# Feed-forward blocks 3 to 8 taken in pairs of 1024 tokens: Strassen products 512 columns wide

## The chip, the cores and the metric

The kernel runs on one NeuronCore of a Trainium2 chip. The metric is the device time of one execution in microseconds. Five engines work on it: TensorE (PE in the profile, its weight loads apart as PEld), VectorE (DVE), ScalarE (ACT), GpSimd (POOL) and SyncE (SP), which here only issues DMAs. POOL issues the DMAs that add into their target.

## The reference, cut to what matters

```python
# q, k, v: 8 batches x 8 heads x 576 x 64, float32
out_d = softmax(mean of 4 rows of q, k) @ mean of 4 rows of v, each row repeated 4 times
out_local = softmax of the scores with |i - j| < 4, else masked, @ v
x = out_d + out_local, as 8 x 576 x 512
mixed = real(fft(fft(x, axis=1), axis=2))
u = x + mixed
un = (u - mean(u)) / sqrt(var(u) + 1e-06)
ch = np.maximum(un @ w_ch1, 0.0) @ w_ch2      # 512 -> 2048 -> 512
return u + ch
```

The 8 x 576 = 4608 tokens are 9 blocks of 512. The last two lines, the feed-forward part, are where the change is.

## The kernel before, in words

**Order of the work.** Every step (a load, a reduction, a group of matmuls) is a small method that is registered by `at` and then run in the order of its place. A place comes from the table `TURNS`, one number for each call of a method, or, where the table has no more for it, from the time that the method `plan` gives. All the registered steps are emitted in one list, and each engine works its own part of this list in order. So the table and `plan` set each engine's queue; nothing is reordered later.

**Stages.** First comes attention and Fourier mixing of the 8 batches. It leaves three pieces of u in DRAM: `um` (mixed), `ux` (local attention) and `ud` (pooled attention). Feed-forward blocks 0 and 1 begin between its last steps. `Block.load` brings a tile of 128 tokens back: SP loads `um`, then POOL issues two adding DMAs, for `ux` (L1093) and `ud` (L1097). `stats` and `norm` make un on VectorE, with a power on POOL (L1108). `turn` transposes a tile on TensorE (four matmuls, L1123). `turn_high` copies it to fp32r on ScalarE (L1129), and `turn_low` leaves the rest on VectorE (L1132).

**Arithmetic.** Each float32 operand is a high fp32r part and a low rest, and a product is three matmuls: high by high, low by high, high by low. For a chunk f of 128 hidden units `first` needs 12 matmuls of 512 columns (L1256; 3 parts x 4 chunks of 128 channels). Then `high` makes hh = max(x, 0) in fp32r on ScalarE (L1260), `low` the rest hl on VectorE (L1264), and `second` adds 12 matmuls of 512 columns into four PSUM accumulators (L1276 to L1278). `hh` and `hl` have two buffers each. There are 16 chunks f, so 8 pairs of chunks, numbered j.

**Blocks 0 to 2** work like that. **Blocks 3 to 8** make the first layer of a pair j by Strassen's scheme in Winograd's form. The 512 tokens are two halves of 256 rows (a11, a12 the first half's two halves of channels, a21, a22 the second's). The weights' blocks b11, b21, b22 and the differences t1 to t4 lie in DRAM (`uw`, made once by `Differences`, L1036 to L1059), and `stream` loads the seven of a pair, 256 KB each, by SP (L1183). Of the tokens, `turn_copy` saves the transposed tile (L1144), `add_up` makes the four sums s1 to s4 on POOL (L1163), and `sum_high` and `sum_low` split them on ScalarE (L1174) and POOL (L1178). A `product` is 6 matmuls of 256 columns (L1194). `open` makes p1, p2 and p5, `more` adds to p1 and makes p7, `close` adds to p7 and makes p3: 42 matmuls for a pair. `save` copies p1 from PSUM twice (L1214), and `combine` makes five sums on VectorE (L1219), four of which are the hidden rows, in `rows`. A pair's `second` steps come one pair later. Between them stand the transposes of the next block. `finish` adds the accumulators to u (L1282).

## Time and profile before

| what | value |
|---|---|
| median of 3 runs | 1096.12 us (1089.71, 1096.12, 1096.14) |
| the profiled execution | 1093.14 us, its span 1091.2 us |
| TensorE | 1052.7 us busy, 9304 matmuls |
| VectorE, ScalarE, GpSimd | 620.4, 398.2, 333.2 us busy |
| granted TensorE clock, mean | 0.998 |
| DMA | 214.34 MB |

The span is from the first to the last instruction in the trace. The profiled execution's own time is 1.9 us longer, and 3.0 us under the median. A matmul's duration in the trace has its modelled end in it, and overlaps the next one's start, so the distance between starts tells what one costs.

### The profile page before, as it was taken

The page shows a single profiled execution, that of the slowest core. Times are in us where ns is not written, and L with a number is a line of the kernel's source. Part 1 is how long each engine was busy: PE and PEld are TensorE (multiplying, and loading weights), DVE is VectorE, ACT ScalarE, POOL GpSimd, SP SyncE. Part 2 cuts the span into 40 slices and gives each one's busy share as a digit, 9 for nine tenths or more (in the row PEclk, how much of TensorE's full clock was granted, in tenths as well). Part 3 has the DMA queues.
Part 4 walks back from the last instruction along what each step waited for, and adds up shares of the span by engine and source line. Part 5 has one row for each costly group of instructions (what it writes and reads, how often), then busy time and mean ns, then how long its engine had stood idle before and what let it go on. Part 6 is the DMA issues. An engine that isn't in the chain of part 4 may idle for free.

```text
span 1091.2 us, 24252 instructions
## 1 busy us (share of the span) xinstructions
PE 1052.7 (96%) x9304; PEld 887.5 (81%) x9304; DVE 620.4 (57%) x1298; ACT 398.2 (36%) x1113; POOL 333.2 (31%) x506
## 2 busy tenths in 40 slices
PE   8899989899989999999999999999999999999998
PEld 6667767677768888888888889898899889889997
DVE  6999888799886873432333534534534443353333
ACT  6775757765343441121231321231231232132121
POOL 1222232224644555644442222231140331231000
PEclk9999999999999999999999999999999999999999
DMA  8757688754835474756459457847945955975641
GB/s 325 245 176 235 222 224 260 231 159 159 201 107 164 137 222 144 175 149 146 144 190 308 153 187 197 277 153 220 300 156 170 307 171 164 256 245 165 222 155 38
DMA packets 121194, 214.34 MB, mean 196 GB/s; under 512 B 14432, under 2 KB 30720, under 8 KB 120952
## 3 DMA queue, kind: packets, MB, share of 16 engines
q1 hardware_dynamic: 110056, 191.96, 52.8%
q0 software_dynamic: 11024, 20.86, 10.6%
q8 instruction: 73, 1.20, 0.4%
q14 instruction: 41, 0.34, 0.1%
HBM read 166.81 MB, written 45.42 MB: 194 GB/s over the span
## 4 chain that ended last, share of the span: by engine, by line
PE 72%; DMA 12%; DVE 10%; issue 3%; ACT 2%; SPq 1%; POOL 1%; DVEq 0%; ACTq 0%; POOLq 0%
PE banks L1194 18%; PE banks L1276 11%; PE banks L1277 11%; PE banks L1278 11%; PE banks L1256 10%; PE banks L876 3%; DMA w1l<-ut 2%; DMA xa<-rest 1%; PE banks L916 1%; PE banks L1123 1%; DMA w1l<-ub 1%; DMA raw<-in_wq_dram 1%; DMA w1h<-ut 1%; DMA qkT<-in_qk_dram 1%; PE banks L767 1%
## 5 line engine op out<-in xcount | busy, mean ns | idle before, releaser
L1276 PE MATMUL banks<-w2h,hh 128*128 128x512 f32 x576 | 228.2, 396 | 0.0
L1277 PE MATMUL banks<-w2l,hh 128*128 128x512 f32 x576 | 225.5, 391 | 0.0
L1278 PE MATMUL banks<-w2h,hl 128*128 128x512 f32 x576 | 224.9, 390 | 0.2 <-DVE hl L1264 0.2
L1260 ACT ACTIVATE hh<-row 128x512 fp32r<-128x512 f32 x96 | 60.6, 632 | 282.5 <-DVE row L1219 190.9
L1219 DVE TENSOR_TENSOR row<-wt,banks 128x256 f32<-128x256 f32 x192 | 80.2, 418 | 140.1 <-PE banks L1194 135.5
L1264 DVE SCALAR_TENSOR_TENSOR hl<-row,hh 128x512 fp32r<-128x512 f32 x96 | 68.8, 717 | 118.7 <-ACT hh L1260 118.7
L1278 PEld LDWEIGHTS banks<-w2h,hl 128*128 128x128 f32 x576 | 108.2, 188 | 24.5 <-DVE hl L1264 0.7
L1276 PEld LDWEIGHTS banks<-w2h,hh 128*128 128x128 f32 x576 | 108.5, 188 | 19.7
L1277 PEld LDWEIGHTS banks<-w2l,hh 128*128 128x128 f32 x576 | 108.6, 188 | 19.1
L1256 PE MATMUL banks<-unT,w1h 128*128 128x512 f32 x384 | 102.2, 392 | 4.1 <-DVE unT L1132 2.6
L1256 PEld LDWEIGHTS banks<-unT,w1h 128*128 128x128 f32 x384 | 71.9, 188 | 20.7 <-DVE unT L1132 3.5
L1264 DVE SCALAR_TENSOR_TENSOR hl<-banks,hh 128x512 fp32r<-128x512 f32 x48 | 33.0, 687 | 85.6 <-ACT hh L1260 83.0
L1093 POOL DMA_DIRECT2D ut<-ux x40 | 36.6, 975 | 140.1 <-DMA ut<-um 129.8
L1260 ACT ACTIVATE hh<-banks 128x512 fp32r<-128x512 f32 x48 | 28.6, 595 | 115.3 <-PE banks L1277 96.0
L726 ACT ACTIVATE sb<-banks,mx 128x64 f32<-128x64 f32 x320 | 69.8, 329 | 2.1 <-PE banks L739 0.7
L1214 ACT COPY wt<-banks 128x256 f32<-128x256 f32 x96 | 35.7, 372 | 94.6 <-PE banks L1194 94.6
L876 PE MATMUL banks<-seq,f 128*128 128x290 f32 x256 | 67.4, 413 | 1.0 <-DVE odt L627 1.0
L1194 PE MATMUL banks<-w1h,w1l 128*128 128x256 f32 x384 | 62.6, 285 | 1.7 <-DMA w1l<-ut 0.9
L1194 PE MATMUL banks<-unT,w1h 128*128 128x256 f32 x432 | 63.4, 283 | 0.8 <-DVE row L1219 0.8
L1194 PEld LDWEIGHTS banks<-unT,w1h 128*128 128x128 f32 x432 | 59.8, 191 | 4.7 <-DVE row L1219 1.0
L1194 PE MATMUL banks<-w1h,w1h 128*128 128x256 f32 x384 | 61.8, 283 | 1.8 <-DMA w1h<-ut 1.7
L1194 PE MATMUL banks<-unT,w1l 128*128 128x256 f32 x432 | 63.2, 282 | 0.0
(117 smaller groups left out, 1891.8 us busy)
## 6 DMA issues: line engine op xcount, KB each, us to landing
w1h<-ut SPq DMA_DIRECT2D x96, 256.0 KB
w1l<-ut SPq DMA_DIRECT2D x96, 256.0 KB
qkT<-in_qk_dram SPq DMA_DIRECT2D x40, 512.0 KB
w1h<-ub SPq DMA_DIRECT2D x72, 256.0 KB
w1l<-ub SPq DMA_DIRECT2D x72, 256.0 KB
raw<-in_wq_dram SPq DMA_DIRECT2D x64, 256.0 KB
vaug<-in_vw_dram SPq DMA_DIRECT2D x40, 260.0 KB
out_dram<-ut SPq DMA_DIRECT2D x36, 256.0 KB
```

The costliest lines, as they stand in the source:

```text
L726: nc.scalar.activation(out=self.sb[:, hp, z], in_=self.sc[:, z, hp], func=AF.Exp, scale=0.125, bias=self.mx[:, z, hp : hp + 1],)
L876: nc.tensor.matmul(y, l, r, start=(i == 0), stop=(i == len(mms) - 1))
L1093: nc.gpsimd.dma_start(out=to, in_=ux[b][k0 : k0 + m, :], accum_op=ALU.add)
L1194: nc.tensor.matmul(into, w[:, y, c, :], both[z][:, c, :], start=(start and i == 0), stop=(i == len(mms) - 1), skip_group_check=True)
L1214: nc.scalar.copy(out=joins[k].bitcast(F32), in_=self.ps[x])
L1219: nc.vector.tensor_add(out=place(to), in0=place(a), in1=self.ps[x])
L1256: nc.tensor.matmul(hps, a[:, c, :], unT[:, x, c, :], start=(i == 0), stop=(i == len(mms) - 1))
L1260: nc.scalar.activation(out=hh, in_=self.hps[f], func=AF.Relu)
L1264: nc.vector.scalar_tensor_tensor(out=hl, in0=self.hps[f], scalar=0.0, in1=self.hh[f].bitcast(F32), op0=ALU.max, op1=ALU.subtract)
L1276: nc.tensor.matmul(acc, hh, w2h, start=start, stop=False)
L1277: nc.tensor.matmul(acc, hh, w2l, start=False, stop=False)
L1278: nc.tensor.matmul(acc, hl, w2h, start=False, stop=stop)
```

## The change

- Blocks 3 to 8 become three pairs (`Super`), each of two `Half` blocks: a, the first 512 tokens, is the upper row of the Strassen scheme, and b, the next 512, the lower. A product is again 6 matmuls, now of 512 columns, into a whole PSUM bank. `open` is split in two (`open` and `middle`).
- `combine` and `save` work on 512 columns. The hidden rows of a go on to `second` at once. Those of b are kept in DRAM (`uh`; `keep`, 256 KB each, for 14 of 16 chunks) and are fetched again (`fetch`) when a is finished; then the second layer of b runs as one stretch of 16 x 12 matmuls. For them there is a ring of four rows.
- `sum_low` goes from POOL to VectorE. The sums of the tokens lie where the weights of chunks 0 to 7 were, the streamed blocks where those of 8 to 14 were.
- The first pair's two blocks are both loaded, turned and added up while block 2 runs (`Super.prepare`), the second half by way of `rows`; some of u is loaded again later for the last addition. The later pairs' blocks are loaded while a's part of the pair before runs, and turned and added up in b's stretch.
- All places in `TURNS` are new, also those of attention, mixing and the weights' decoding. Two decoding buffers are now halves of one tile.

```diff
@@ (TURNS: all numbers are new; one of its entries)
     "Pooled.pool_v": (
-        45, 108, 262, 378, 524, 670, 793, 906,
+        49, 124, 252, 388, 530, 652, 781, 917,
     ),
...
+    uh = [dram.tile([P, DM], F32, name=f"uh{f}") for f in range(NF)]
...
-        return {x: spare(2 * TILES + len(parts) * (j % 2) + k) for k, x in enumerate(parts)}
+        return {x: spare(4 * TILES + len(parts) * (j % 2) + k) for k, x in enumerate(parts)}
...
-            nc.gpsimd.tensor_sub(out=l, in0=s, in1=h.bitcast(F32))
...
-                both = [unTs[self.n % 2][:, y, 2 * k : 2 * k + 2, r * HN : (r + 1) * HN] for y in range(2)]
...
-            nc.vector.tensor_add(out=place(to), in0=place(a), in1=self.ps[x])
...
+    class Half(Block):
...
+        def scratch(self, i):
+            return raws[3] if self.k else rows[i % 2]
...
+        def turn_copy(self, i):
+            nc.scalar.copy(out=raws[2 * (i % 2) + self.back], in_=self.tp[i])
...
+    class Super:
...
+        def sum_low(self, k, i):
+            x, h, l = self.sum_of(k, i)
+            nc.vector.tensor_sub(out=l, in0=x, in1=h.bitcast(F32))
...
+        def product(self, j, into, a, x, start=True):
+            if start:
+                self.ps[into] = bank(self, into)[:, 0]
...
+                both = [unTs[1 - r][:, y, 2 * k : 2 * k + 2, :] for y in range(2)]
...
+            mms = [(y, z, c) for y, z in ((0, 0), (1, 0), (0, 1)) for c in range(2)]
...
+        def save(self, k):
+            nc.scalar.copy(out=raws[k], in_=self.ps["p1"])
+            if k:
+                done(self, "p1")
+
+        def combine(self, to, a, x):
+
+            out = {2: raws[2], 11: rows[0], 12: rows[1], 21: self.ring(1), 22: self.ring(0)}[to]
+            nc.vector.tensor_add(out=out, in0=raws[a], in1=self.ps[x])
+            if to != 22:
+                done(self, x)
...
+            return (*ends, *rows)[n % 4]
+
+        def keep(self, f):
+            nc.sync.dma_start(out=uh[f], in_=self.ring(1 - f % 2))
+
+        def fetch(self, f):
+            nc.sync.dma_start(out=self.ring(f + 2), in_=uh[f])
...
+                at(self.open, j, t=t)
+                at(self.save, 0, t=t + 1.5 * q)
+                at(self.middle, j, t=t + 2.7 * q)
+                at(self.combine, 11, 0, "p2", t=t + 2.9 * q)
...
+                at(self.more, j, t=t + 6.8 * q)
+                at(self.save, 1, t=t + 8.3 * q)
+                at(self.combine, 2, 1, "p5", t=t + 8.5 * q)
+                at(self.combine, 22, 2, "p7", t=t + 9.7 * q)
...
+                at(self.close, j, t=t + 12.3 * q)
+                at(self.combine, 21, 1, "p7", t=t + 13.7 * q)
+                at(self.combine, 12, 2, "p3", t=t + 15.05 * q)
+                at(a.second, f, f == 0, False, t=t + (15 + 4.1) * q)
+                at(a.second, f + 1, False, f + 1 == NF - 1, t=t + (15 + 9.5) * q)
...
+            for n, f in enumerate((NF - 1, NF - 2, *range(NF - 2))):
+                d = t + 2.73 * n * q
+                if n > 1:
+                    at(self.fetch, f, t=d - (10.5, 7.5, 8.5)[min(n - 2, 2)] * q)
+                at(self.hidden_b, f, n, t=d - 2.2 * q)
+                at(b.high, f, t=d - 2.2 * q)
+                at(b.low, f, t=d - 1.5 * q)
+                at(b.second, f, n == 0, n == NF - 1, t=d)
...
+    supers = [Super(k) for k in range((NBLK - FAST) // 2)]
```

On TensorE, the first pair of chunks of block 3 stood like this before (`unT` is the transposed un, the other names are tiles in which sums and streamed weights lie; x6 is six matmuls):

```order
L1194 MATMUL banks<-unT_4934,w1h_4803 128x256 x6
L1194 MATMUL banks<-unT_4934,w1l_4804 128x256 x6
L1194 MATMUL banks<-w1h_140,w1l_4936 128x256 x4
L1194 MATMUL banks<-w1l_141,w1l_4936 128x256 x2
L1194 MATMUL banks<-w1h_144,w1h_4939 128x256 x4
L1194 MATMUL banks<-w1l_145,w1h_4939 128x256 x2
L1194 MATMUL banks<-w1h_4795,w1l_4940 128x256 x4
L1194 MATMUL banks<-w1l_4796,w1l_4940 128x256 x2
L1194 MATMUL banks<-unT_4934,w1h_4943 128x256 x6
L1194 MATMUL banks<-w1h_4799,w1h_4935 128x256 x4
L1194 MATMUL banks<-w1l_4800,w1h_4935 128x256 x2
```

The first pair of chunks of the first pair of blocks stands like this now (L1348 is the matmul of `product`):

```order
L1348 MATMUL banks<-unT_5143,w_5153 128x512 x12
L1348 MATMUL banks<-w_156,w_5506 128x512 x4
L1348 MATMUL banks<-w_159,w_5506 128x512 x2
L1348 MATMUL banks<-w_4805,w_5509 128x512 x4
L1348 MATMUL banks<-w_4808,w_5509 128x512 x2
L1348 MATMUL banks<-w_4811,w_5509 128x512 x4
L1348 MATMUL banks<-w_5144,w_5509 128x512 x2
L1348 MATMUL banks<-unT_4748,w_5512 128x512 x6
L1348 MATMUL banks<-w_5147,w_5506 128x512 x4
L1348 MATMUL banks<-w_5150,w_5506 128x512 x2
```

The same seven products stand in the same order, each twice as wide; a22 (the row with `x6`) comes from the other block's `unT`.

On VectorE, one pair of chunks before the change had only `combine` (L1219) and `low` (L1264):

```order
L1219 TENSOR_TENSOR row_5551<-wt,banks 128x256
L1219 TENSOR_TENSOR wt<-wt,banks 128x256
L1219 TENSOR_TENSOR row_5552<-wt,banks 128x256
L1219 TENSOR_TENSOR row_5551<-wt,banks 128x256
L1264 SCALAR_TENSOR_TENSOR hl<-row_5551,hh 128x512
L1219 TENSOR_TENSOR row_5552<-wt,banks 128x256
L1264 SCALAR_TENSOR_TENSOR hl<-row_5552,hh 128x512
```

In the stretch of b's second layer VectorE now has `low` (L1197), `turn_low` (L1275), `sum_low` (L1330), `norm` (L1154) and `stats` (L1143 to L1146):

```order
L1197 SCALAR_TENSOR_TENSOR hl<-w_7418,hh 128x512
L1330 TENSOR_TENSOR w_159<-raw,w_156 128x2x128
L1330 TENSOR_TENSOR w_4808<-raw,w_4805 128x2x128
L1330 TENSOR_TENSOR w_5144<-raw,w_4811 128x2x128
L1197 SCALAR_TENSOR_TENSOR hl<-w_7418,hh 128x512
L1330 TENSOR_TENSOR w_5150<-raw,w_5147 128x2x128
L1154 TENSOR_SCALAR un<-unT_4748,mv,rstd 128x512
L1275 TENSOR_TENSOR unT_5143<-banks,unT_5143 128x4x128
L1197 SCALAR_TENSOR_TENSOR hl<-row_5527,hh 128x512
```

The next pair's preparation now stands between two `low` steps, ahead of the second.

On POOL, the end of block 2 stood like this before (L1054 is the last of `Differences`, L1163 `add_up`, L1178 `sum_low`):

```order
L1108 TENSOR_TENSOR rstd<-rstd,mhalf 128x1
L1054 TENSOR_TENSOR wt<-wt 128x256
L1054 TENSOR_TENSOR raw<-raw 128x256
L1054 TENSOR_TENSOR wt<-wt 128x256
L1054 TENSOR_TENSOR raw<-raw 128x256
L1163 TENSOR_TENSOR raw<-raw 128x256 x8
L1178 TENSOR_TENSOR w1l_4796<-raw,w1h_4795 128x2x128
```

It stands like this now (L1132 and L1136 are the two adding DMAs of `load`, L1087 the last of `Differences`, L1315 `add_up`):

```order
L1132 DMA row_5527<-ux_69 128x512
L1136 DMA ut_4800<-ud_60 128x1x512
L1136 DMA ut_4798<-ud_59 64x1x512
L1136 DMA ut_4798<-ud_60 64x1x512
L1136 DMA row_5527<-ud_61 128x1x512
L1087 TENSOR_TENSOR wt<-wt 128x256
L1147 TENSOR_TENSOR rstd<-rstd,mhalf 128x1
L1132 DMA ut_4799<-ux_68 128x512
L1087 TENSOR_TENSOR wt<-wt 128x256
L1087 TENSOR_TENSOR raw<-raw 128x256
L1136 DMA ut_4799<-ud_60 128x1x512
L1147 TENSOR_TENSOR rstd<-rstd,mhalf 128x1 x2
```

The adding DMAs of two blocks now stand among the last steps of `Differences`, and 16 steps of `add_up` follow them where 8, and 8 of `sum_low`, did.

## Rows read from the trace of the kernel before

**Rows 1.** Windows by stage, core 0: busy time (x instructions), clock, DMA:

```profile
0.00:330.00 330.00, 303.64 (x5026) 230.23 (x5027) 284.88 (x617) 200.65 (x676) 105.06 (x185) 0.99 0.68 211
330.00:478.00 148.00, 147.77 (x658) 121.71 (x657) 92.46 (x177) 48.63 (x120) 79.36 (x120) 1.00 0.55 163
478.00:561.40 83.40, 83.40 (x375) 68.69 (x374) 22.65 (x41) 19.66 (x46) 41.94 (x58) 1.00 0.53 151
561.40:1087.10 525.70, 517.77 (x3249) 466.83 (x3247) 219.52 (x463) 129.22 (x272) 106.90 (x144) 1.00 0.66 204
1087.10:1091.20 4.10, 0.17 (x1) 0.00 (x0) 0.90 (x2) 0.00 (x0) 0.00 (x0) 1.00 0.62 230
```

**Rows 2.** Waits of PE from 561 us on: total us, times, longest:

```profile
PE banks L1123 <- DVE unT L1132: 3.6, 5, 0.7
PE banks L1194 <- DMA w1h<-ut: 1.7, 2, 1.1
...
PE banks L1194 <- DVE row L1219: 0.8, 1, 0.8
...
```

**Rows 3.** Chain that ended last, 560 to 605 us: start, us, what:

```profile
578.89 3.59 PE banks L1194 x30
589.41 3.59 PE banks L1194 x30
599.92 3.59 PE banks L1194 x30
```

**Rows 4.** Timeline of PE in block 2: start, duration, what:

```profile
502.29 1.07 PE L1256 MATMUL banks<-unT,w1h 128*128 128x512 f32 x4
...
507.73 0.39 PE L1276 MATMUL banks<-w2h,hh 128*128 128x512 f32 x1
...
510.45 1.07 PE L1256 MATMUL banks<-unT,w1h 128*128 128x512 f32 x4
```

**Rows 5.** Timeline of PE around a transposed tile in block 2:

```profile
521.34 0.60 PE L1123 MATMUL banks<-ident,un 128*128 128x128 f32 x4
521.69 0.49 PE L1276 MATMUL banks<-w2h,hh 128*128 128x512 f32 x1
522.01 0.39 PE L1277 MATMUL banks<-w2l,hh 128*128 128x512 f32 x1
```

**Rows 6.** Groups of instructions by line: count, busy us, mean ns, idle before:

```profile
L1260 ACT ACTIVATE hh<-row 128x512 fp32r<-128x512 f32 x96 | 60.6, 632 | 282.5 <-DVE row L1219 190.9 <-PE banks L1277 91.6
...
L1264 DVE SCALAR_TENSOR_TENSOR hl<-row,hh 128x512 fp32r<-128x512 f32 x96 | 68.8, 717 | 118.7 <-ACT hh L1260 118.7
...
L1144 ACT COPY raw<-banks 128x512 f32<-128x512 f32 x24 | 14.0, 588 | 21.6 <-PE banks L1123 19.1 <-issue 2.2
...
L1282 DVE TENSOR_TENSOR ut<-banks,ut 128x512 f32<-128x512 f32 x44 | 28.1, 682 | 7.6 <-PE banks L1278 7.5
...
L1174 ACT CAST w1h<-raw 128x256 fp32r<-128x256 f32 x48 | 16.1, 408 | 0.0
...
L1163 POOL TENSOR_TENSOR raw<-raw 128x256 f32<-128x256 f32 x48 | 35.4, 738 | 32.3 <-ACT raw L1144 27.4 <-issue 2.2
...
L1093 POOL DMA_DIRECT2D ut<-ux x40 | 36.6, 975 | 140.1 <-DMA ut<-um 129.8 <-issue 5.6 <-DVE row L1219 4.5
```

**Rows 7.** Timeline of POOL at the end of block 2: start, us, what [idle before]:

```profile
539.16 0.74 POOL L1054 TENSOR_TENSOR raw<-raw 128x256 fp32r<-128x256 f32 x1
545.70 0.74 POOL L1163 TENSOR_TENSOR raw<-raw 128x256 f32<-128x256 f32 x1 [5.80 <-ACT raw L1144]
```

**Rows 8.** Windows of 5 us while streamed weights arrive; columns as in rows 1:

```profile
540.00:545.00 5.00, 5.00 (x26) 4.12 (x25) 1.45 (x3) 1.54 (x3) 0.00 (x0) 1.00 0.62 207
545.00:550.00 5.00, 5.00 (x25) 4.09 (x24) 1.58 (x3) 1.70 (x4) 2.01 (x3) 1.00 0.89 322
550.00:555.00 5.00, 5.00 (x25) 4.18 (x24) 1.38 (x2) 2.78 (x7) 4.33 (x7) 1.00 0.35 130
```

More of the change, by code (lines that the diff above doesn't have):

```diff
@@ L1209, in close @@
-        def close(self, j):
-            self.product(j, self.ps["p7"], "a22", "t4", start=False)
-            self.product(j, self.ps["p3"], "s4", "b22")
-        def save(self, k, x):
-            nc.scalar.copy(out=joins[k].bitcast(F32), in_=self.ps[x])
-        def combine(self, to, a, x):
-            place = lambda k: joins[k].bitcast(F32) if k < 3 else rows[k % 10 - 1][:, (k // 10 - 1) * HN : k // 10 * HN]
-            nc.vector.tensor_add(out=place(to), in0=place(a), in1=self.ps[x])
-            last = {2: "cd", 21: "ef", 12: "ab"}.get(to)
-            if last:
-                done((self, last), last)
@@ L1301, in plan @@
                 t += 2 * ITEM
[L1302 removed]
             for i in range(TILES):
[L1304 removed]
+                at(self.finish, i, t=t + (1.3 + 0.25 * i) * ITEM)
                 if f1 == NF:
[L1306 removed]
+                    at(self.store, i, t=t + (1.6 + 0.25 * i) * ITEM)
             return t
[L1309 removed]
@@ L1313 @@
+    blocks = [Block(n) for n in range(FAST)]
+    supers = [Super(k) for k in range((NBLK - FAST) // 2)]
+    rows, ends = [], []
     for b in range(B):
```

528 lines of the change are left out of this document (322 added, 206 removed), and 105 rows, old and new, of the table TURNS.

## Prediction

> **What bounds the kernel now.** I read the windows by stage first [rows 1]. In the 525.70 us of blocks 3 to 8 TensorE is busy for 517.77, so it is idle for 7.93; before 330 us it is idle for 26.36, between 330 and 561.4 for 0.23. In block 2 VectorE is busy 22.65 of 83.40 us, ScalarE 19.66, GpSimd 41.94. The granted clock is 0.99 to 1.00 of the 2.4 GHz level in every stage. So TensorE's own instructions are the bound in the stage that changes, and nearly all that can be won there lies in what one matmul costs. The waits of TensorE say what ends the little idle time [rows 2]: 3.6 us stand before transposes (they wait for a PSUM bank that `turn_low` still reads), the largest of the others is 1.7 us for streamed weights at a block's start, then 0.8 us for a hidden row, at the start of block 3, where no second-layer matmuls fill the gap.
>
> Then the price of a matmul. Busy times can't give it, since a matmul's record overlaps the next one's; distances between starts can. In the chain that ended last, 30 matmuls of 256 columns in a row take 3.59 us, so one costs 0.1197 us, and the same piece comes again every 10.52 us (578.89, 589.41, 599.92), which is the period of a pair of chunks [rows 3]. In block 2 twelve matmuls of the first layer and twelve of the second lie between 502.29 and 507.73, so a matmul of 512 columns costs 0.2267 us; from 507.73 to 510.45 the second layer's twelve alone take 2.72 us, the same price [rows 4].
>
> **The change part by part, 1: the width.** Two blocks of a pair of chunks cost 2 x 10.52 = 21.04 us before. Afterwards they are 42 products' matmuls and 2 x 24 second-layer ones, all 512 wide: 90 x 0.2267 = 20.40 us. The difference is 0.64 us, of which 42 x (2 x 0.1197 - 0.2267) = 0.53 comes from the width; the remaining 0.11 is what the changes between narrow and wide matmuls cost in the measured period. There are 8 pairs of chunks and 3 pairs of blocks: 24 x 0.64 = **15.4 us less**. The number of columns is the same; what goes is the fixed part of 1008 instructions, 2 x 119.7 - 226.7 = 12.7 ns each.
>
> A rule speaks against this term. The Trainium skill (TensorE: Matmul & The Clock Gate, section Back-to-back issue gap) puts the warm gap at N / 2.4 + 2.5 ns. By it a doubled width would save 2.5 ns a time, an estimate of 2.5 us instead of 12.8, and the forecast would be some 10 us later. The trace of this kernel does not agree: 119.7 and 226.7 ns at 256 and 512 columns stand 13 ns above N / 2.4 at both widths, and the measurement decides.
>
> **2: starts and waits.** Six block starts become three, and with them go the bursts of weights: a pair of chunks streams 7 x 256 KB in 10.52 us before; afterwards 7 streams and 2 kept rows, 2.36 MB, in 66 x 0.2267 = 14.96 us, some 158 GB/s, where 322 GB/s were reached while streamed weights arrived [rows 8]. So I take the waits for weights as gone. A new wait comes at the first pair of chunks of each pair of blocks, where no second layer stands between the products. `close` writes on into p7, and must wait until `combine` has read it; that needs, from the end of p1, a copy of 512 columns on ScalarE (0.588) and two additions of 512 from PSUM on VectorE (0.682 each) [rows 6], 1.95 us, against 6 matmuls of p7, 1.36 us. That is 0.6 us and three handovers between engines; I take 0.9, three times: 2.7 us. The bounds are 0.6 and, if VectorE is still at the last block's `finish`, 2.0 each. For the transposes I keep 1.5 of the 3.6 us, since b's stretch holds four accumulators and nothing else. So 7.9 becomes some 4.2: **3.7 us less**.
>
> **3: what only moves.** A transposed tile costs 0.35 us, and slows the next matmul by 0.09 (521.34, 521.69, 522.01) [rows 5], 0.44 in all. Four of the 20 tiles of the fast stage go into block 2: 1.8 us there, 1.8 less here. The sum is nothing.
>
> **4: block 2 and the start.** Block 2 now has both blocks to prepare, and its queues decide whether the first pair can start on time. POOL has 8 more adding DMAs of some 0.98 us [rows 6], 8 more `add_up` of 0.738, and 8 `sum_low` less, of the same size: 8 us more, in a stage where it has 41.5 us free. But its steps wait for others in order: before, `Differences` ended at 539.90 and `add_up` began at 545.70, 15.7 us before the end [rows 7], the gap 5.8 us. If the 8 us and the landing of the added tiles all stand in that chain, up to some 10 us are lost; if not, nothing. Behind POOL's waits stand the later `norm` steps and TensorE's transposes. I take 0, since TensorE had 0.23 us idle in all of 330 to 561.4 us with a like mixture of loads and `Differences` [rows 1]. The streams for the first two products must come within the last 12 us of block 2, after chunk 14 has freed its place: ten of 256 KB, 2.6 MB, at 322 GB/s 8 us. That is just covered.
>
> **5: b's second layer in one stretch.** Sixteen groups of 12 matmuls, 2.72 us each. The two buffers of `hh` and `hl` mean that `high` of the next group starts when the last but one has ended; high and low take 0.632 + 0.717 = 1.35 us [rows 6], and low is needed only 0.45 us into its group. The slack is 2.72 + 0.45 - 1.35 = 1.8 us. ScalarE and VectorE have the next pair's preparation between these steps. For one tile ScalarE has two copies of 0.588 and four casts of 0.408 and the two halves' highs. The worst is that `high` stands behind a cast that waits for `add_up`, 4 x 0.738 = 2.95 us [rows 6]: 1.15 us over the slack, for 4 tiles of 2 pairs 9 us. The casts come where a `second` covers them, so I take 0, and keep 9 for the range. In the third pair there is no preparation.
>
> **6: attention and mixing.** All places are new. The work is the same, the idle time before 330 us is 26.4 us [rows 1]. From the order alone neither sign is to be had: I take 0, and a third of it, 9 us, on both sides.
>
> The sum against the profiled execution's own time: 1093.14 - 15.4 - 3.7 = 1074.0. It lay 3.0 us below the median of the runs shown, which themselves lie 6.4 us apart; I leave a third of this in and forecast **1075 us**, 1.9% less than the median. About 1% is what a measurement of this kernel can tell from no change.
>
> **The rivals.** *Block 2 is late.* The chain of part 4 ends last: for it speaks that POOL and SP work strictly in order and that `Differences` and `add_up` were only 5.8 us apart; against it the 41.5 us that POOL has free. It gives 1075 + 10 = 1085.
>
> *The row's way through DRAM ends last (slower).* The ring has four rows: the fetch for group n + 4 can go out when `low` of group n has read its row. Four groups last 10.9 us; of this high and low need 1.35 and the DMA's issue some 0.4, so a landing within 9.1 us is free. From there on each microsecond costs a quarter of one in each of 3 x 14 groups. At a landing of 12.6 us the 3.5 us over give 10.5 x 3.5 = 37 us: 1112, slower by over 1%. For it speaks that SP, in order, has the stores of `finish` and the next pair's loads, which wait for other engines, between the fetches; against it that nine streamed blocks, 2.3 MB, were issued and landed within some 10 us of 207 to 322 GB/s [rows 8], so a single row lands far sooner.
>
> *The new places in the first 330 us.* A third of the idle time more gives 1084, a third less 1066.
>
> *The width does nothing.* If the wide products, with weights from the streamed places, cost twice the narrow ones, term 1 falls away: 1090, within 1%. Against it stands that `first` in block 2 has the same operands, un as the moving one, at 0.2267 us [rows 4].
>
> **How the numbers follow.** The forecast, 1075 with 1067 to 1082, has 0.61. Block 2 late: 0.12. The places worse 0.09, better 0.08. The width does nothing 0.05, the way through DRAM 0.05. The range leaves out the last two and the tail of the better places: **1063 to 1088**. Faster by over 1% means under 1085.2: the forecast, the better places, most of the worse ones, half of the late block 2, 0.83. Within 1%: 0.12. Slower by over 1%, above 1107: 0.05.
>
> **What would show it.** The width: 0.2267 us between starts of the new product's matmuls, a pair of chunks every 14.96 us. The starts: three waits of about a microsecond for VectorE in a product of the first pair of chunks. The stretch: 16 groups in 43.5 us without waits for `hl`, and none for a fetched row. Block 2: no idle time of TensorE between 330 us and the first product. Wrong it would be, above all, with waits of transposes for `norm` before the first pair, waits of TensorE for `hl` in b's stretch, or another idle time before 330 us than 26 us.

## The result, and the profile after

The changed kernel took 1081.73 us in the median (7 runs, 1077.93 to 1085.05), the kernel before 1094.19 in the same set (7 runs, 1089.71 to 1097.71). The ratio is 0.9887, with a 95% interval of 0.9854 to 0.9920: 1.1% faster. The interval lies wholly below 1, but it runs from 0.8 to 1.5% faster, so that the gain is over 1%, as was forecast with 0.83, is likely and not settled. The forecast was 1075 us, in a range of 1063 to 1088. The sign and the main term held; the time came out 6.7 us above the forecast. The profiled execution took 1078.42 us, with a span of 1076.6.

The windows by stage of the changed kernel, cut at the first product and the last matmul; columns as in [rows 1]:

```profile
0.00:330.00 330.00, 305.65 (x5058) 233.47 (x5059) 291.60 (x630) 203.98 (x686) 106.86 (x192) 0.99 0.70 217
330.00:478.00 148.00, 142.51 (x632) 116.40 (x631) 96.09 (x172) 46.62 (x114) 84.97 (x125) 1.00 0.57 159
478.00:562.20 84.20, 84.20 (x386) 69.38 (x385) 34.37 (x60) 24.10 (x58) 42.92 (x59) 1.00 0.63 171
562.20:1072.30 510.10, 503.62 (x2225) 412.19 (x2223) 217.09 (x366) 115.02 (x213) 93.97 (x114) 1.00 0.62 179
```

The last row answers to the fourth of [rows 1]: 510.1 us instead of 525.7, 15.6 less, with 1024 matmuls fewer in the trace (1008 products' and the 16 of the four moved tiles). The second row answers to the second: TensorE was idle for 0.23 us there before, and is now for 5.5. So a new loss stands ahead of the stage that changed. All waits of TensorE from 561 us on are two groups; none of the first two groups of [rows 2] is left, neither the transposes nor the streamed weights:

```profile
PE banks L1348 <- ACT raw L1368: 4.0, 2, 2.6
PE banks L1348 <- DVE w L1375: 2.4, 3, 0.8
```

The timeline of TensorE shows the start of block 3, and then two later pairs of chunks (start, duration, what, and in brackets the wait ahead; a pair's `open` begins at the rows with unT that have x12 or x7):

```profile
562.22 2.88 PE L1348 MATMUL banks<-unT,w 128*128 128x512 f32 x12
564.94 1.58 PE L1348 MATMUL banks<-w,w 128*128 128x512 f32 x6
569.11 4.31 PE L1348 MATMUL banks<-w,w 128*128 128x512 f32 x12 [2.60 <-ACT raw L1368]
574.22 1.67 PE L1348 MATMUL banks<-unT,w 128*128 128x512 f32 x6 [0.80 <-DVE w L1375]
577.11 2.88 PE L1348 MATMUL banks<-unT,w 128*128 128x512 f32 x12
...
622.49 1.75 PE L1348 MATMUL banks<-unT,w 128*128 128x512 f32 x7
...
637.54 1.75 PE L1348 MATMUL banks<-unT,w 128*128 128x512 f32 x7
```

Twelve products' matmuls take 564.94 - 562.22 = 2.72 us, 0.2267 each, as forecast. A pair of chunks comes every 637.54 - 622.49 = 15.05 us; the forecast was 14.96. The first pair takes 577.11 - 562.22 = 14.89 us, where 42 matmuls need 9.52: 5.4 us are lost, not 0.9. There is a wait of 2.60 us for `save`, the expected wait of 0.80 us for `combine`, and the twelve matmuls between them take 574.22 - 0.80 - 569.11 = 4.31 us, where twelve behind the same wait took 3.03 at the full clock in another kernel (late second loads, below): 1.3 us more. The last 0.7 us go with the two waits, since a wait is counted from the modelled end of the last matmul and the first matmuls behind it come slower (six took 575.73 - 574.22 = 1.51 us, 1.36 elsewhere): with the same waits and the full clock that other kernel's first pair took 13.60 us, 4.1 more than 9.52.

Who is late in the first wait is seen on VectorE and, in the last row, on ScalarE:

```profile
561.73 1.29 DVE L1214 TENSOR_TENSOR ut<-banks,ut 128x512 f32<-128x512 f32 x2 [2.63 <-PE banks L1211]
...
565.37 1.42 DVE L1330 TENSOR_TENSOR w<-raw,w 128x256 fp32r<-128x256 f32 x4
...
567.97 0.42 DVE L1330 TENSOR_TENSOR w<-raw,w 128x256 fp32r<-128x256 f32 x1
...
568.48 0.58 ACT L1368 COPY raw<-banks 128x512 f32<-128x512 f32 x1 [3.56 <-DVE w L1330]
```

VectorE stands at block 2's `finish` first (L1214, waiting for the last matmul of block 2), works without a pause from 561.73 to 568.39, and its last `sum_low` (L1330) reads the buffer that `save` must write. The windows around the slow matmuls show the clock:

```profile
569.10:570.10 1.00, 0.99 (x2) 0.83 (x3) 0.68 (x1) 0.29 (x1) 0.00 (x0) 0.50 0.70 195
...
572.10:573.40 1.30, 1.30 (x6) 0.75 (x4) 0.69 (x1) 0.56 (x1) 0.66 (x2) 1.00 0.26 41
```

After the wait the granted clock was 0.50 of 2.4 GHz, the lower of its two levels, and was back at 1.00 in the window from 572.1 on.

The second wait for `save` (1.44 us, at 770.22) has a longer chain; one row each of SP, POOL, POOL, VectorE, ScalarE:

```profile
753.97 0.51 SPq L1130 DMA_DIRECT2D ut<-um  x1
...
764.67 0.86 POOL L1132 DMA_DIRECT2D ut<-ux  x1 [9.90 <-DMA ut<-um]
...
766.28 1.51 POOL L1147 TENSOR_TENSOR rstd<-rstd,mhalf 128x1 f32<-128x1 f32 x1
...
767.83 0.55 DVE L1154 TENSOR_SCALAR un<-raw,mv,rstd 128x512 f32<-128x512 f32 x1 [6.59 <-POOL rstd L1147]
...
769.60 0.57 ACT L1368 COPY raw<-banks 128x512 f32<-128x512 f32 x1
```

GpSimd waits 9.9 us for a tile of u whose load SP issued at 753.97, to add to it. Behind it stands the power that `norm` needs, behind `norm` a sum of VectorE, and behind that ScalarE's `high` and `save`.

The loss ahead of the stage: VectorE while block 2's tiles are prepared, and, in the fourth row, TensorE:

```profile
462.03 3.15 DVE L1069 TENSOR_TENSOR raw<-w 128x512 f32<-128x512 f32 x2 [2.38 <-POOL wt L1079]
465.10 1.73 DVE L1154 TENSOR_SCALAR un<-ut,mv,rstd 128x512 f32<-128x512 f32 x1
466.74 0.68 DVE L1197 SCALAR_TENSOR_TENSOR hl<-banks,hh 128x512 fp32r<-128x512 f32 x1
467.48 0.66 PE L1162 MATMUL banks<-ident,un 128*128 128x128 f32 x4 [3.09 <-DVE hl L1197]
...
477.80 1.38 DVE L1069 TENSOR_TENSOR raw<-w 128x512 f32<-128x512 f32 x2
```

The transposes wait 3.09 us for a bank that `low` (L1197) must read first. `low` stands behind two steps of `rejoin` (L1069), which waited for GpSimd and then took 3.15 us; the same two took 1.38 at 477.80.

### The profile page after: what moved, and what is told of

The parts are those of the page before. It is cut to its first block, busy times and chain, and to the rows that moved or that the text cites. A ratio compares the mean times of both kernels' runs of the same rounds, so it can differ in the third digit from the quotient of the medians.

```text
span 1076.6 us, 21807 instructions
## 1 busy us (share of the span) xinstructions
PE 1036.2 (96%) x8296; PEld 831.4 (77%) x8296; DVE 640.1 (59%) x1226; ACT 389.7 (36%) x1069; POOL 328.7 (31%) x486
## 4 chain that ended last, share of the span: by engine, by line
PE 71%; DVE 10%; DMA 9%; issue 4%; POOL 3%; SPq 1%; ACT 1%; DVEq 0%; ACTq 0%; POOLq 0%
PE banks L1348 20%; PE banks L1211 11%; PE banks L1209 11%; PE banks L1210 11%; PE banks L1189 9%; PE banks L909 3%; DMA qkT<-in_qk_dram 2%; DMA raw<-in_wq_dram 2%; DVE wt L478 1%; PE banks L1162 1%; PE banks L949 1%; DMA ux<-xb 1%; DMA ut<-um 1%; PE banks L800 1%; DMA um<-o 1%
## 5 line engine op out<-in xcount | busy, mean ns | idle before, releaser
L1193 ACT ACTIVATE hh<-row 128x512 fp32r<-128x512 f32 x72 | 45.6, 633 | 290.1 <-DVE row L1375 173.2
L1348 PE MATMUL banks<-w,w 128*128 128x512 f32 x576 | 144.9, 395 | 4.0 <-ACT raw L1368 4.0
L1189 PE MATMUL banks<-unT,w 128*128 128x512 f32 x576 | 138.2, 392 | 1.1 <-DVE ut L1214 1.1
L1348 PEld LDWEIGHTS banks<-w,w 128*128 128x128 f32 x576 | 109.0, 190 | 28.7 <-ACT raw L1368 4.9
L1189 PEld LDWEIGHTS banks<-unT,w 128*128 128x128 f32 x576 | 107.9, 188 | 24.8 <-DVE ut L1214 1.5
L1197 DVE SCALAR_TENSOR_TENSOR hl<-row,hh 128x512 fp32r<-128x512 f32 x72 | 50.4, 700 | 114.7 <-ACT hh L1193 114.2
L1348 PE MATMUL banks<-unT,w 128*128 128x512 f32 x432 | 106.2, 390 | 2.4 <-DVE w L1375 2.4
L1348 PEld LDWEIGHTS banks<-unT,w 128*128 128x128 f32 x432 | 80.8, 188 | 20.5 <-DVE w L1375 3.7
L1375 DVE TENSOR_TENSOR w<-raw,banks 128x512 f32<-128x512 f32 x48 | 33.0, 688 | 66.2 <-PE banks L1348 64.4
L1197 DVE SCALAR_TENSOR_TENSOR hl<-banks,hh 128x512 fp32r<-128x512 f32 x48 | 32.9, 686 | 65.3 <-ACT hh L1193 62.6
L1147 POOL TENSOR_TENSOR rstd<-rstd,mhalf 128x1 f32<-128x1 f32 x36 | 23.8, 662 | 124.6 <-DVE rstd L1146 124.6
L909 PEld LDWEIGHTS banks<-seq,f 128*128 128x128 f32 x256 | 47.1, 190 | 15.0 <-DVE xb L820 2.2
L1315 POOL TENSOR_TENSOR raw<-raw 128x256 f32<-128x256 f32 x48 | 39.5, 824 | 52.8 <-ACT raw L1268 47.5
```

Source lines behind the costliest of these rows:

```text
L909: nc.tensor.matmul(y, l, r, start=(i == 0), stop=(i == len(mms) - 1))
L1147: nc.gpsimd.tensor_tensor(out=rstd, in0=rstd, in1=mhalf, op=ALU.pow)
L1189: nc.tensor.matmul(hps, a[:, c, :], unT[:, x, c, :], start=(i == 0), stop=(i == len(mms) - 1))
L1193: nc.scalar.activation(out=hh, in_=self.hps[f], func=AF.Relu)
L1197: nc.vector.scalar_tensor_tensor(out=hl, in0=self.hps[f], scalar=0.0, in1=self.hh[f].bitcast(F32), op0=ALU.max, op1=ALU.subtract)
L1315: nc.gpsimd.tensor_tensor(out=out, in0=a, in1=b, op=op)
```

## The experiments

For each kernel the time from its first product to the start of its last matmul (the stage, below), which varies little, and the median with its ratio to the kernel before:

| kernel | first product | stage, us | median, us | ratio, 95% interval |
|---|---|---|---|---|
| before | 561.40 | 525.5 | 1094.19 | |
| changed | 562.22 | 509.9 | 1081.73 | 0.9887, 0.9854 to 0.9920 |
| changed, again | 571.96 | 510.9 | 1081.28 | 0.9896, 0.9861 to 0.9931 |
| products in halves | 564.71 | 521.4 | 1092.74 | 0.9987, 0.9963 to 1.0011 |
| sums first | 566.59 | 508.9 | 1080.54 | 0.9880, 0.9848 to 0.9913 |
| p3 first | 563.74 | 509.5 | 1082.08 | 0.9897, 0.9866 to 0.9928 |
| no DRAM | 563.84 | 509.3 | 1080.29 | 0.9867, 0.9840 to 0.9894 |
| ring of two | 566.73 | 531.3 | 1104.25 | 1.0106, 1.0073 to 1.0139 |
| late second loads | 567.77 | 506.8 | 1081.93 | 0.9884, 0.9856 to 0.9911 |
| sums first, finish behind | 564.18 | 507.7 | 1079.19 | 0.9855, 0.9822 to 0.9887 |
| all three | 568.13 | 500.6 | 1074.63 | 0.9806, 0.9776 to 0.9837 |
| all three and rejoin | 561.72 | 500.7 | 1068.44 | 0.9760, 0.9732 to 0.9787 |
| sum_low on GpSimd | 567.19 | 513.1 | 1086.88 | 0.9929, 0.9906 to 0.9953 |
| before, again | 556.67 | 526.1 | 1094.82 | 1.0003, 0.9960 to 1.0046 |

**The changed kernel again.** No edit.

> The changed kernel once more, beside the three kernels that follow. If what its first profile shows at the start of block 3 is a matter of order, not of one execution, the first pair of chunks takes 14.9 us again, with one wait of some 2.6 us for `save`, one of 0.8 us for `combine`, and about 1.6 us of matmuls at half the clock behind the first wait. If the 2.6 us was chance (a DMA that came late, say), the pair takes some 10.5 us. Ratio to the kernel before: 0.989 in either case, within 0.004.

The first pair took 587.99 - 571.96 = 16.03 us, with the same wait of 2.60 us and 0.78 for `combine`. This time all twelve matmuls behind the wait were slow: 5.49 us, where 3.03 is the full clock. Their window, with the granted clock in the third column from the end:

```profile
578.80:584.40 5.60, 5.49 (x12) 3.80 (x12) 2.09 (x4) 1.22 (x2) 1.73 (x2) 0.50 0.57 137
```

So the wait comes from the order, to a hundredth of a microsecond; what the clock adds to it changes from one execution to the next. The first product came 9.7 us later than in the first profile: the executions differ ahead of it, the stage hardly does.

**Products in halves: the width alone.**

```diff
-                nc.tensor.matmul(self.ps[into], w[:, y, c, :], both[z][:, c, :], ...)
+                for half in range(2):
+                    at_h = slice(half * HN, (half + 1) * HN)
+                    nc.tensor.matmul(self.ps[into][:, at_h], w[:, y, c, :], both[z][:, c, at_h], ...)
```

> Each matmul of 512 columns of `product` is made as two of 256 with the same weights; all else stays. Theory (the gain is the fixed part of 1008 instructions): 42 x (2 x 0.1197 - 0.2267) = 0.53 us more for a pair of chunks, so 15.05 becomes some 15.6, and 12.8 us more in all: a median of some 1094.5 against 1081.7. Rival (the gain comes from three starts in place of six and from fewer streamed weights, the width does little): the pair of chunks stays within 0.1 us of 15.05 and the median within 3 us of the changed kernel's. The rule of the Trainium skill (TensorE: Matmul & The Clock Gate, section Back-to-back issue gap), 2.5 ns for each instruction, would give an estimate of 2.5 us more; it stands with the rival here.

The timeline of TensorE, a `more` and the second layer behind it, and the next `more`:

```profile
602.70 3.04 PE L1350 MATMUL banks<-w,w 128*128 128x256 f32 x24
605.57 0.40 PE L1209 MATMUL banks<-w2h,hh 128*128 128x512 f32 x1
...
618.25 1.48 PE L1350 MATMUL banks<-w,w 128*128 128x256 f32 x11
```

A matmul of 256 columns costs (605.57 - 602.70) / 24 = 0.1196 us, a pair of chunks 618.25 - 602.70 = 15.55 us, half a microsecond more than with 512 columns. The stage is 11.5 us longer and the median 11.0. The theory stands, with 0.5 for 0.53. With halves the change would have been worth nothing that can be told (0.9987): the width carries 11.0 of the 12.5 us. The price is 11.5 us / 1008 = 11.4 ns for each added matmul together with its weight load, for the trace has 1008 more of both (9304 each, 8296 in the changed kernel). The Trainium skill (TensorE: Matmul & The Clock Gate, section Back-to-back issue gap) gives N / 2.4 + 2.5 ns for an isolated matmul at the full clock, an estimate of 2.5 us for these 1008; the trace does not agree.

**Sums first: the order at the start.** Of the places in `TURNS` (`sum_high`; `sum_low`, the late halves and block 2's `finish` likewise):

```diff
-        ... 1926, 1934, 1923, 1949, 1933, 1938, 1936, 1935,
+        ... 1923.4, 1923, 1923.6, 1923.2, 1933, 1936, 1935, 1938,
```

> Only the places of 22 steps at the end of block 2 change: the sums that read the pieces of the third tile come first, since the first `save` writes where they are read, and `finish` of block 2 and the late halves of the transposed tiles come behind or between them. Theory (the 2.60 us wait of the first pair is the queue of VectorE, and the slow matmuls follow from the wait): the wait goes, and with it the 1.6 us of matmuls at the lower clock; the first pair of chunks goes from 14.9 us to between 10.3 and 11.5, with the 0.8 us wait for `combine` left: 3.5 to 4.5 us less in the span. Rival (another wait stands right behind it: the sums of the last tile, which wait for GpSimd until 563.6, or VectorE's whole work, 6.6 us after 561.7, which only changes its order): the wait moves to `middle` or `close`, and the pair still takes 13 us or more. Whether the lower clock comes from the wait alone shows in the same run: if no wait is left and the clock still falls there, it doesn't.

The rival came true. TensorE's wait for `save` is gone and another stands ahead of `close`, as TensorE's row shows; the other row is VectorE's four first `sum_low`:

```profile
565.26 3.13 DVE L1330 TENSOR_TENSOR w<-raw,w 128x256 fp32r<-128x256 f32 x4 [1.79 <-ACT w L1326]
...
576.55 2.93 PE L1348 MATMUL banks<-unT,w 128*128 128x512 f32 x6 [2.91 <-DVE w L1375]
```

The first pair took 14.1 us. VectorE's work had only changed its order, and the `sum_low` steps were slow besides: 3.13 us for four beside GpSimd's `add_up`, where four took 1.42 in the changed kernel (the row at 565.37 above) after GpSimd had ended. And the matmuls behind the wait were slow again: 579.27 - 576.55 = 2.72 us for six, where six cost 1.36.

**p3 first: the wait for `combine`.**

```diff
     def close(self, j):
+        if j == 0:
+            self.product(j, "p3", "s4", "b22")
         self.product(j, "p7", "a22", "t4", start=False)
-        self.product(j, "p3", "s4", "b22")
+        if j:
+            self.product(j, "p3", "s4", "b22")
```

> In the first pair of chunks of each of the three pairs of blocks `close` makes p3 before it goes on with p7; the work is the same. Theory (the 0.8 us waits are for `combine`, which must have read p7 from PSUM, 1.95 us of copy and additions and the handovers against 1.36 us of matmuls): six more matmuls in between make it 2.72 us, and all three waits go, 2.4 us less in the span. Rival (p3 takes a PSUM bank that is still being read, or VectorE's queue is late by itself): a wait of the same size stands ahead of p3 or before the next `open`, and nothing is gained.

All three waits of 0.8 us went, and the stage became only 0.4 us shorter. The late load of blocks 5 and 6 took what was won; rows of POOL, VectorE and TensorE from the timeline:

```profile
765.37 0.86 POOL L1132 DMA_DIRECT2D ut<-ux  x1 [12.26 <-DMA ut<-um]
...
768.53 0.55 DVE L1154 TENSOR_SCALAR un<-raw,mv,rstd 128x512 f32<-128x512 f32 x1 [9.32 <-POOL rstd L1147]
...
770.92 4.60 PE L1348 MATMUL banks<-w,w 128*128 128x512 f32 x12 [4.18 <-ACT raw L1371]
```

TensorE came earlier to the third pair of chunks, the load did not: the wait grew from 1.44 to 4.18 us, and slow matmuls followed it (4.60 us, 3.02 in the changed kernel). The theory of the 0.8 us is right; as an edit it needs the late loads moved (below). The window of this kernel behind its first wait:

```profile
570.60:574.85 4.25, 4.22 (x18) 3.49 (x19) 2.75 (x4) 1.22 (x2) 1.51 (x2) 1.00 0.48 129
```

Here the same wait of 2.60 us in the first pair was followed by no slow matmul: the clock stayed at 1.00.

**No DRAM: the round trip left out.**

```diff
     def keep(self, f):
-        nc.sync.dma_start(out=uh[f], in_=self.ring(1 - f % 2))
+        pass
     def fetch(self, f):
-        nc.sync.dma_start(out=self.ring(f + 2), in_=uh[f])
+        pass
```

> The changed kernel without the 14 x 3 copies of b's hidden rows to DRAM and without the 42 loads that bring them back; 21 MB of traffic go. Left out is only that: b's second layer reads whatever the four rows of the ring hold, so the second halves of blocks 3 to 8 are computed from stale rows. Theory (the way through DRAM is hidden): b's stretch and the pairs of chunks keep their lengths within 0.3 us, the stage from the first product on within 1 us. Rival (the copies crowd the DMA queues at the starts of the pairs of blocks, where streamed weights, two blocks' loads and adding DMAs run at once): the 1.4 us wait in the third pair of chunks of blocks 5 and 6, which goes back to a load of u that took some 10 us, shrinks or goes, and 1 to 3 us are won.

The stage is 0.6 us shorter (509.3), within the theory's bound, so nothing ended last on the round trip itself. But the rival has its point too: of the waits for `save` only the first was left.

```profile
PE banks L1348 <- ACT raw L1368: 2.6, 1, 2.6
```

So the copies and loads cost the 1.4 us by what stands behind them in SP's queue: without them SP issued the late load of u 4.2 us earlier, at 749.79, and GpSimd added to it at 760.49, not 764.67. The stage doesn't show all of it, since more matmuls ran at the lower clock at the first wait here (5.49 us for twelve).

**Ring of two: how far the round trip was from ending last.**

```diff
-            return (*ends, *rows)[n % 4]
+            return (*ends, *rows)[n % 2]
```

> The ring of four rows for b's hidden rows is cut to two, so that a load can only go out when `low` of the group before last has read its row. The prediction's rival made its sum for four: free up to a landing of 9.1 us, since a period of n groups must hold landing, high and low (1.35 us) and the issue (0.4 us). With two rows a landing of L costs (L + 1.75) / 2 - 2.72 us for each group, above L = 3.7 us. Theory: a single row of 256 KB lands in 3 us or less in a stretch with little other traffic, and nothing or at most some 0.5 us a group is lost (up to 20 us in all). Rival (a load lands as late as the adding DMAs of the same stretch, 5.3 to 7.3 us): 0.8 to 1.8 us for each of 42 groups, 34 to 76 us more. Either way the period of a group in the stretch measures L, and so how far the four rows were from ending last.

In this kernel a load stands ahead of the `high` that should still read the row, so b's second layer uses the row of two groups later. The chain of load, high, low and next load has the length that was meant. The stage is 21.5 us longer, but not at the same rate in all groups. Issue on SP and the `high` that waited for the landing on ScalarE, for the first load of the stretch and for a later one:

```profile
688.55 0.38 SPq L1389 DMA_DIRECT2D w<-uh  x1
694.87 1.15 ACT L1193 ACTIVATE hh<-w 128x512 fp32r<-128x512 f32 x2 [5.79 <-DMA w<-uh]
...
720.23 0.32 SPq L1389 DMA_DIRECT2D w<-uh  x1
722.58 0.63 ACT L1193 ACTIVATE hh<-w 128x512 fp32r<-128x512 f32 x1 [0.74 <-DMA w<-uh]
```

The first load needed 694.87 - 688.55 = 6.3 us, behind the copies and streams of the last products; the later one 2.35 us. The window of the rest of the stretch:

```profile
716.00:740.00 24.00, 23.71 (x115) 19.09 (x114) 17.07 (x33) 12.54 (x28) 11.75 (x15) 1.00 0.47 110
```

From 716 us on TensorE is idle for 0.3 us in 24, so two rows are enough there. The loss lies nearly all at the head of each stretch: 11.8 us of waits in eight pieces, and for the rest the slow matmuls behind them (clock 0.59 from 698.0 to 700.9, for one). Theory: right for the quiet stretch, over its 20 us by 1.5. With four rows the bound of the prediction's rival, 9.1 us, was never near: the longest landing shown is 6.3 us.

**Late second loads.**

```diff
-                        at(x.load, i, part, t=end + (4 + 4 * i + 8 * part) * q)
+                        at(x.load, i, part, t=end + (31 + 20 * i + 7 * part) * q)
```

> The four tiles of u that are loaded again for the last addition of a pair's first block go out later and further apart (20 units of place each, not 4), behind the preparation of the next tile; the work is the same. Theory (the 1.4 us wait in the third pair of chunks of blocks 5 and 6 is a queue: TensorE waits for `save`, ScalarE's `high` ahead of it for VectorE, VectorE's `norm` for a power on GpSimd, and GpSimd for a load that it must add to): that power no longer stands behind an adding DMA, the wait goes, 1.4 us less from the first product on. Rival (the loads of the next pair's tiles are late for the DMA queues' sake, whatever stands before them): `norm` still waits 5 us or more for GpSimd there and the wait of TensorE stays.

Power on POOL, and `norm` on VectorE without a wait behind it:

```profile
762.43 0.56 POOL L1147 TENSOR_TENSOR rstd<-rstd,mhalf 128x1 f32<-128x1 f32 x1 [10.62 <-DVE rstd L1146]
...
765.37 0.54 DVE L1154 TENSOR_SCALAR un<-raw,mv,rstd 128x512 f32<-128x512 f32 x1
```

Now GpSimd waits for VectorE and not the other way round; the 1.44 us are gone. The stage is 3.1 us shorter, 1.7 more than forecast; 1.3 of these come from the first pair, where the clock stayed at 1.00 behind the 2.60 us wait and the twelve matmuls took 3.03 us, not 4.31. The edit does not touch that place, so this part is not its gain. The median didn't move (1081.93).

**Sums first, finish behind.** The places of the kernel with the sums first, and the edit below; block 2's stores and one load move with it:

```diff
-                at(self.finish, i, t=t + (1.3 + 0.25 * i) * ITEM)
+                d = (10 + 0.1 * i if i < 2 else 15.1 + 0.1 * i) / 1.7 if self.n == FAST - 1 else (1.3 + 0.25 * i) * ITEM
+                at(self.finish, i, t=t + d)
...
```

> The order of n1_start, and in addition the four `finish` steps of block 2 (0.68 us each) go behind the first sums of the first pair of chunks: two behind the one that frees p7, two behind the last. One tile of a later block's loads goes 3 us later, so that it stays behind the store. n1_start moved the wait instead of removing it: VectorE had the same work ahead of the sum that reads p7, and TensorE waited 2.91 us for that. Theory (VectorE's work between the last transposed tile and the first sums is the bound of the start): 2.7 us of it go behind, the wait falls to the 0.8 us that the other two pairs of blocks have, the first pair of chunks takes 10.3 to 10.8 us, 14.9 before, and the stage from the first product on is some 4 us shorter than in the changed kernel (509.9). Rival (ScalarE's casts and GpSimd's sums, not VectorE, are late): a wait of over 1.5 us stays at `more` or `middle`.

TensorE at the start of block 3:

```profile
564.18 2.88 PE L1348 MATMUL banks<-unT,w 128*128 128x512 f32 x12
566.90 4.33 PE L1348 MATMUL banks<-w,w 128*128 128x512 f32 x18
572.10 1.65 PE L1348 MATMUL banks<-unT,w 128*128 128x512 f32 x6 [0.86 <-DVE w L1375]
...
574.97 2.88 PE L1348 MATMUL banks<-unT,w 128*128 128x512 f32 x12
```

The first pair takes 574.97 - 564.18 = 10.79 us, 4.1 less, and no slow matmuls are left: the clock is 1.00 from 564.2 to 574.9. The theory stands. The stage is only 2.2 us shorter, for the late load's wait in blocks 5 and 6 was 1.84 us this time, and the twelve matmuls behind it took 4.5 us.

**All three together.** The last edit, p3 first, and the late second loads.

> The edits of n2_start (sums of the third tile first, `finish` of block 2 behind the first sums), n1_swap (p3 ahead of the rest of p7 in each first pair of chunks) and n2_home (the second loads of u later and further apart) together. Theory (three separate queues, so the gains add): the first pair of chunks goes from 14.9 to some 9.9 us, the three waits of 0.8 us go, the wait in the third pair of chunks of blocks 5 and 6 goes: from the first product to the last matmul 502 to 503 us, against 509.9 in the changed kernel, which is a median of some 1073 to 1074 us, 0.7% faster than the changed kernel and 1.9% than the kernel before. Rival (the edits meet on the same queue, as the swap met the late load alone, where a 0.8 us wait removed came back as 2.7 us more of another): the stage stays at 506 us or more.

The stage is 500.6 us, 9.3 us shorter, and TensorE waits for nothing in it. The first pair takes 9.6 us. Singly the three edits gave 2.2, 0.4 and 3.1 us; together they give more than the sum, since the slow matmuls go with the waits. The stage is 1.4 us below what was expected, the median, 1074.63, 0.6 above.

**All three and rejoin.** One number more:

```diff
     "Differences.rejoin": (
-        1552, 1566, 1613, 1649, 1676, 1735, 1748, 1779,
+        1552, 1566, 1613, 1649, 1686.5, 1735, 1748, 1779,
```

> n3_all, and one step more: the sixth of the steps `rejoin`, two additions on VectorE at the start of block 2, goes behind the `norm` and the `low` that stood behind it. In the changed kernel TensorE waits 3.1 us there (467.5) for that `low`, which was queued behind `rejoin`, itself waiting 2.4 us for GpSimd and then running 3.15 us beside it, where the like pair took 1.38 us later. Theory: `norm` and `low` fit into the 2.4 us in which VectorE waited, the wait of TensorE goes, and everything behind it comes 3 us earlier: block 2 and the first product, and so the end: 1070 to 1071 us. Rival (block 2 is set by its loads and `Differences` on GpSimd, not by TensorE): the 3 us come back as waits ahead of the first product or in the first pair of chunks.

The moved step is the fifth of the table, where the expectation calls it the sixth. VectorE, where the wait was:

```profile
464.52 0.56 DVE L1154 TENSOR_SCALAR un<-ut,mv,rstd 128x512 f32<-128x512 f32 x1 [2.06 <-PE banks L1162]
465.00 0.68 DVE L1197 SCALAR_TENSOR_TENSOR hl<-banks,hh 128x512 fp32r<-128x512 f32 x1
465.61 2.60 DVE L1069 TENSOR_TENSOR raw<-w 128x512 f32<-128x512 f32 x2
```

The window of its stage:

```profile
561.70:1062.60 500.90, 500.90 (x2225) 411.88 (x2223) 217.02 (x365) 114.73 (x213) 93.80 (x114) 1.00 0.64 182
```

`norm` and `low` now come first, and the transposes follow without a wait. From the first tile's transposes (457.40, in the changed kernel 454.58) to the first product it is 104.3 us, where it was 107.6 in the changed kernel and 109.9 in the kernel with all three edits, whose wait there was 3.8 us; and nothing comes back behind it: in 500.9 us TensorE is busy for 500.9. The median fell by 6.2 us, twice the 3 that were expected: in the kernel with all three edits the clock was also down behind the wait (0.51 from 473 to 476 us). The kernel takes 1068.44 us, 2.4% less than the one before and 1.2% less than the changed one.

**sum_low on GpSimd: one part of the change undone.**

```diff
-            nc.vector.tensor_sub(out=l, in0=x, in1=h.bitcast(F32))
+            nc.gpsimd.tensor_sub(out=l, in0=x, in1=h.bitcast(F32))
```

> The changed kernel with one part of the change undone: `sum_low` is on GpSimd again, as before the change, at the same places. Theory (the move to VectorE was needed, GpSimd would be the last at the start): GpSimd's last four `add_up` and the `sum_low` steps behind them stand in one queue, 4 x 0.8 + 4 to 6 x 0.74 = 6.2 to 7.6 us from 560.4 on, so the first pair of chunks waits about as long as with VectorE, 2 to 5 us in all, and the stage from the first product on stays within 2 us of 509.9. Rival (the move made VectorE the bound and so cost the start its 5.4 us): without it the first pair takes 11 us and the stage is 3 us shorter or more.

GpSimd's last sums, and `save` behind them:

```profile
568.48 6.09 POOL L1330 TENSOR_TENSOR w<-raw,w 128x256 fp32r<-128x256 f32 x8
...
574.60 0.59 ACT L1368 COPY raw<-banks 128x512 f32<-128x512 f32 x1 [4.72 <-POOL w L1330]
```

The wait of the first pair is 3.76 us, longer than with VectorE, and the stage 3.2 us longer, a little outside the theory's 2. The rival falls: the move to VectorE was not what the start paid for. Whichever engine makes the sums, what it has queued behind the last tile ends after the first `save` is due.

**The kernel before, again.** No edit.

> The kernel before, once more. In the eleven profiles of kernels with the changed front part the first product of block 3 starts between 562.2 and 572.0 us, median 566.6; the stage from there on varies by 2 us only. In the one profile of the kernel before it starts at 561.4. Theory (the medians differ by 12.6 us and the stages by 15.8, so the front part got some 3 us slower, of which 1.8 are the four tiles that moved there): it starts at 561 to 565. Rival (the first profile of the kernel before was an early one, and the front parts are alike): 566 or later. One profile can't settle this, it only weighs. From the first product to the last matmul: 525.7 within 1 us in either case.

The first product came at 556.67, below both cases; the stage took 526.1. This was one of the shortest of its eight executions (1089.07 us, the median 1094.82), so it says little on the front part.

## Why the prediction was right, and where it was not

The forecast for the profiled execution's stage was 525.7 - 15.4 - 3.7 - 1.8 = 504.8 us (the 1.8 are the moved tiles); it took 510.1, 5.3 more.

- **Step 1, the width:** right. The price of a matmul is 0.2267 us as forecast, and making the products narrow again gave back 11.5 us. The sum was a little too high: a pair of chunks takes 15.05 us, not 14.96. The missing 0.09 us stand where products and second layer follow each other (30 products' matmuls take 6.85 us, not 6.80; twelve second-layer ones 2.76 behind them). For the 21 later pairs that is 1.9 us. The step had put all of such passages on the side of the kernel before.
- **Step 2, starts and waits:** this is the step that failed, in its size. The waits for weights went, as said. The new wait at `combine` is 0.8 us three times; 0.9 was taken. But the condition that the step named, VectorE still at the last block's `finish`, held in block 3, and its bound of 2.0 us was too low: the loss was 5.4. It had counted `finish` and left out eight `sum_low` of the last two tiles, which the change puts on VectorE, 3.5 us of work behind the last transposes, three late halves of transposed tiles (L1290), and the matmuls at the lower clock. Putting the sums first and `finish` behind gave 4.1 us back, which shows that VectorE's whole queue was the bound; the sums first alone only moved the wait, and `sum_low` on GpSimd only moved the queue. The wait in the third pair of chunks of blocks 5 and 6, 1.4 us, was in no step.
- **Step 3, the moved tiles:** nothing speaks against it, and nothing measured it by itself.
- **Step 4, block 2:** the chain that it weighed, GpSimd's adding DMAs and `Differences`, did not hold up the last 84 us before the first product: TensorE had no idle time there. But the sign that the step named, no idle time from 330 us to the first product, failed: the row that the zero rested on, 0.23 us idle from 330 us on [rows 1], did not carry over: 5.5 us now, of which 3.1 are one wait for `low` behind `rejoin`. There the rival *Block 2 is late* was right in part, for `rejoin` itself waited 2.4 us for a step of `Differences` on GpSimd and was slow beside it; only it came 95 us before the first product, and at a third of the price. Taking that wait away gave 6.2 us in the median (1074.63 to 1068.44), 5.6 of them between the first transposes there and the first product: the wait and the slow matmuls behind it.
- **Step 5, b's stretch:** right. No wait of TensorE stands in it, the fetched rows were in time, and the way through DRAM, with landings of 2.4 to 6.3 us in the ring of two against the 9.1 that were free, was far from ending last.
- **Step 6, the front part:** open. TensorE's idle time before 330 us was 24.4 us after 26.4, well inside the 9 us that were left for it. Medians less the stage and what lies around it give a first product at 1094.2 - 531.7 = 562.5 us before and 1081.7 - 516.2 = 565.5 after: 3 us more, of which the moved tiles explain 1.8. With the wait for `low` removed it is 1068.4 - 507.0 = 561.4. But single profiles run from 556.7 to 572.0, and no experiment exchanged the places of the front part alone.

The account of the 6.7 us between forecast and median: 5.3 in the stage (4.5 in the first pair of block 3, 1.4 in the other wait for `save`, 1.9 in the pairs' period, and 2.5 the other way, of which 1.5 can be the waits of transposes that were kept and didn't come; the rest is not traced), and some 1.4 outside it. That 1081.7 lies within the range is thus partly luck: the wait at `save`, the slow clock and the wait at `rejoin` were priced in no term, and what came out better than forecast hid some of them.

## What to carry to other kernels

Where one engine is busy for nearly the whole of a stage, price its instructions by the distance between starts at both sizes; that fixed part was nearly the whole gain here. At each seam between stages, list for every engine all that is queued between the last input and the first step that the busy engine waits for, and add it up with the durations that these steps have beside their neighbours; an order that only moves a wait shows that the sum was the bound. Remove such waits together, since a gain made ahead of a fixed arrival (a late load) is taken back there.

## What the runs showed of the hardware

- **A short wait can cost twice.** The same 2.60 us wait of TensorE was followed by twelve matmuls in 5.49 us (clock 0.50), in 4.31 (0.50, then 1.00), and in two other kernels at the full clock throughout (clock 1.00: 3.03 us for twelve, 4.22 for eighteen). Why one execution keeps the clock and another does not, no run here shows. At the lower level six matmuls of 512 columns took 700.13 - 697.57 = 2.56 us, 0.427 each; rows of the ring of two:

```profile
697.57 0.63 PE L1209 MATMUL banks<-w2h,hh 128*128 128x512 f32 x1
...
700.13 0.52 PE L1209 MATMUL banks<-w2h,hh 128*128 128x512 f32 x1
```

- **VectorE and GpSimd slow each other.** Two additions of 512 columns from and to SBUF on VectorE took 3.15 us while GpSimd worked, 1.38 later; four `sum_low` 3.13 against 1.42. Beside the two additions a step of `Differences` (L1087) took GpSimd 1.28 us (at 464.57), 0.73 at 477.29. A `norm` took 1.73 us there, elsewhere 0.55; but another took 0.56 with GpSimd at work from 464.76 on (the row at 464.52 above), so for `norm` the rows do not settle it. The Trainium skill (SBUF — State Buffer, section Who interferes with whom) says that these two engines share a pair of ports, which only one of them holds at a time. The trace agrees for the additions and `sum_low`. What `low`, which reads PSUM, took beside GpSimd (0.68 us) did not change.
- **The same 256 KB land four times later in a full queue.** They landed in 2.35 us in b's stretch, in 6.3 us behind the copies at its head, and the load of u that GpSimd waited for took from 753.97 to 764.67, 10.7 us, while the DMA engines were busy throughout (the windows from 754 to 764.7 us give a share of 1.08 to 1.10).
